# One core, cosine attention into a gated MLP: first-pair norms of four units by a power on GpSimd, and reciprocals of the odd units' sums by ScalarE straight from PSUM

## The chip, the cores and the metric

The kernel runs on one core of one Trainium2 chip. The metric is the device time of one execution in microseconds (us). The core has five engines that run side by side and wait for each other through semaphores: TensorE (PE in the profile; PEld is its weight load), ScalarE (ACT), VectorE (DVE), GpSimd (POOL) and SyncE (SP), whose queue here only issues DMAs. Each engine, and each issuing queue, takes its instructions strictly in the order in which the program holds them.

## The reference

The first part is attention over cosine similarities, the second an MLP with the gate h·cos(h). Eight batches, 12 heads, 448 positions, 64 numbers a head.

```python
q_n = q / (np.linalg.norm(q, axis=-1, keepdims=True) + 1e-06)
k_n = k / (np.linalg.norm(k, axis=-1, keepdims=True) + 1e-06)
scores = np.matmul(q_n, k_n.transpose(0, 1, 3, 2)) / tau
attn = np.exp(scores - max);  attn = attn / (sum(attn) + 1e-09)
attn_out = np.matmul(attn, v)                      # (8, 12, 448, 64)
x = attn_out as (8*448, 12*64)
h = x @ w_in;  g = h * np.cos(h);  out = g @ w_out  # (3584, 768)
```

## The kernel before

**Units and pairs.** The work on heads is cut into 16 units `u` of six heads (half a batch), and each unit into three pairs of heads, numbered `g = 3u + p` from 0 to 47. A batch `b` is units `2b` and `2b + 1`.

**Norms of a unit** (`square`, `reduce`, `rnorm`, `scale`). GpSimd squares q and k of a pair (L617, 1.7 us), VectorE sums the squares over a head (L624), and 1/norm is made in one of two ways. Most units take ScalarE: a `Ln` (L644) and an `Exp` with scale -0.5 (L647), one instruction each for all three pairs of the unit (42 columns). Unit 3 takes GpSimd: it adds 1e-12 (L640) and raises to the power -0.5 (L641), pair by pair (14 columns). GpSimd then multiplies q and k by it (`scale`, L655, 1.7 us a pair, tile `qks`). From pair 9 on, a transposing DMA on SP's queue (L672, labels `T9`, `T10`, ...) brings `qks` into `qkT`, which the scores of that pair read. The norms of unit `u + 1` are made while the pairs of unit `u` are worked on.

**A pair** (`pair`, `scores`, `attend`). TensorE makes the scores of pair `g` in four steps (the first, a narrow one, at L712, three at L704) into two PSUM buffers SC, ScalarE takes the exponential of each (L719, tile `PX`), and TensorE multiplies by the values of pair `g - 1` into PSUM tile AV (L741 and L733; L793 and L809 for the pairs below). The sums over the exponentials, the softmax denominators, are made in two ways. Pairs in `PLAN["direct"]` (0 to 5, 7 to 11, 17, 23, 47) make them beside the product, and ScalarE inverts them from PSUM by `Ln` and `Exp` with scale -1 (L873 and L875; L859 and L861 for pairs 0 to 3). The other pairs of a unit share a count step (`counts`, L765): TensorE multiplies by a matrix of ones at chosen columns (`mark`, L558 to L562), so that each sum lands in a row of AV.

**The chain of a unit** (`counts`, then `chain`). VectorE copies the 128x224 sums out of AV into `xs` (L771). A DMA on SP's queue gathers 16 rows of `xs` (four, where only one pair is left) into `sums`, spread over 128 partitions of 28 columns (L892). VectorE takes the reciprocal (L899; for unit 2 GpSimd, L896). A second DMA writes it to the DRAM buffer `scr` (L900, `spread`), two more read it back, broadcast to 64 partitions each, into `RB` (L902, `bcast`). GpSimd multiplies the unnormalized products `xu` by `RB` into `xT` (L907), one instruction a pair.

**The MLP.** M1 of a batch (`m1`, L920) multiplies `w_in` by `xT`; ScalarE takes a sine with a shift (the cosine, L949) and VectorE the product `g` (L951). M1 of batch `b` stands behind the pair at `points[...]`: pairs 12, 21, 27, 33, 39, 45 for batches 1 to 6, and the end for batch 7. For its sines ScalarE loads another function table (L534) ahead of M1 and the exponential's table behind it, and in between there is no `Ln` or `Exp`. M2 (L1019 in quarters of the array, L1048 whole) multiplies by `w_out`. Its steps are put between the steps of the pairs in counted portions (`m2_fill`), each tile's result is copied out (L983, L986) and stored (L990).

**What sets the order.** The kernel's code lists the operations with what they read and write, and a list scheduler (`Program.arrange`, `play`) then gives each engine its fixed order from estimated costs. Each operation has a latest start (`late`) reckoned backwards from TensorE's own order; an engine other than TensorE takes the ready operation with the earliest `late`. TensorE keeps the written order except that it may look eight steps ahead for one that is ready. So an edit to one operation can move others on any engine.

Of the kernel before, what the change touches and what calls it, by code (L numbers as in the profile page):

```python
# [6 lines left out]
ACT = mybir.ActivationFunctionType  # L7
ALU = mybir.AluOpType
# [5 lines left out]
PLAN = {  # L14
    "apart": 1,
    "ahead": (1, 2),
    "halves": tuple(range(25)),
    "folded": (0, 1, 2, 3),
    "grid": {2: (16, 5, 6), 3: (11, 3, 4), 4: (8, 2, 3)},
    "hold": 0.6,  # L20
    "margin": 1.0,
    "sq": ["AA", "A", "A", "P", "P", "P"],
# [4 lines left out]
    "late4": {1: (7, "T9"), 2: (8, "T10")},  # L27
    "power": (2,),
    "late": 0.0,
    "sooner": {8: 20, 12: 20},  # L30
    "mixed": (3, (3, 0, 1, 2, 0, 1, 2, 0), (2, 3, 4, 0, 1, 5)),
    "turned": 9,
# [9 lines left out]
    "turns": {3: (3, 0, 1, 2, 0, 1, 2, 0)},  # L42
    "lastbank": 2,
    "end": (4, 3, 0),
    "parts": {3: (0, 1, 2, 3), 4: (0, 1, 3)},
    "scaled": {},
    "squared": {(5, 2): "A"},
    "u5": ("gather2", "gather2", "gather2"),
    "tail": 192,
    "twin": 4,  # L50
    "given": {13:(0,0,2,3),16: (4, 0, 5, 2), 22:(1,2,5,6), 26:(3,2,5,6), 27:(0,0,3,2), 34: (12, 4, 5, 6), 46: (12, 4, 3, 4), 47: (4, 0, 5, 0)},
    "roots": (3,),
    "lead": {33: 5, 45: 5, 12: 13, 21: 13},
    "vloads": {3: [(4, "x6"), (5, "x6")], 4: [(6, "x11")], 5: [], 6: [(7, "x15"), (8, "x15")]},
    "behind": {2: 8, 3: 0, 4: 8},
# [340 lines left out]
def bass_cosine_attention__then__act_gcu_kernel(  # L396
# [9 lines left out]
    B, NH, S, D = q.shape  # L406
# [53 lines left out]
    xs = sbs("xs", 2, [128, S // 2], F32)  # L460
    RB = sbs("RB", 2, [128, UP * S], F32)
    sums = sbs("sums", 2, [128, S // 16], F32)
    rcp = sbs("rcp", 2, [128, S // 16], F32)
# [5 lines left out]
    mark = sb("mark", [128, 3 * 4 * 32], BF16)  # L469
    iot = cosb[0].bitcast(I32).ap()[:, 0:128]  # L470
    cst = sb("cst", [128, 4], F32)
# [7 lines left out]
    scr = nc.dram_tensor("scr", (NU, 8 * S), F32)  # L479
# [11 lines left out]
    markv = mark.ap().rearrange("p (k v m) -> p k v m", k=3, v=4)  # L491
# [5 lines left out]
    AVv = AV.ap().rearrange("p (a s) -> p a s", a=2)  # L497
# [13 lines left out]
    def dma(eng, fns, reads, writes, sem, bulk=0.0, label="", behind=None, weight=1.0, pad=0.0):  # L511
        took, descs = 0.75, 0
        for y in ISSUE if eng == "SP" else ():
            if label.startswith(y):
                took, descs = ISSUE[y]
        o = P.op(eng, lambda e: [f(e) for f in fns], reads, writes, cost=took * len(fns), dma=sem, bulk=bulk, label=label)
        o.nd, o.descs, o.lead = len(fns), descs * len(fns), 0.3 if label[0] == "T" else 0.0
        o.weight, o.pad = weight, pad
        if behind is not None:
            P.order_only(behind, o)  # L520
        return o
# [3 lines left out]
    def act(fn, reads, writes, cols, table=None, aps=0, label="", bias=0.0):  # L525
        o = P.op("ACT", fn, reads, writes, cost=0.165 + cols / 1200.0 + 0.09 * aps, label=label, bias=bias)
        if table is not None:
            if last_table[0] is not None:
                P.order_only(last_table[0], o)
            last_table[1].append(o)  # L530
        return o
# [9 lines left out]
    def dve(fn, reads, writes, cycles, lock=False, label="", bias=0.0):  # L541
        return P.op("DVE", fn, reads, writes, cost=0.15 + cycles / 960.0, lock=lock, label=label, bias=bias)

    def pool(fn, reads, writes, cost, label="", bias=0.0):
        return P.op("POOL", fn, reads, writes, cost=cost, lock=True, label=label, bias=bias)
# [13 lines left out]
    for z in range(2):  # L559
        for n, at in enumerate(((0, 24), (0, 16, 24), (8,), (16,))):  # L560
            for x in at:
                dve(lambda e, z=z, n=n, x=x: e.memset(markv[64 * z : 64 * z + 64, 0 : z + 2 : z + 1, n, x : x + 1], 1.0), ["mark0"], ["mark"], 8)  # L562
    sel = [gT.bitcast(F32).ap()[:, (f * RING + S) // 2 : (f * RING + S) // 2 + 128] for f in (NF - 2, NF - 1)]
    for n in range(2):
        dve(lambda e, n=n: e.tensor_scalar(
# [65 lines left out]
    def rnorm(u, p0, p1, t=(0, 1)):  # L631
        i = u % 2
        h, w = slice(2 * p0, 2 * p1), slice(*blocks(t))
        n = (p1 - p0) * 2 * (w.stop - w.start)
        tag = "%d.%d" % (u, p0) + ("" if len(t) == 2 else "ab"[t[0]])
        keys = [(p, z) for p in range(p0, p1) for z in t]
        if u in PLAN["roots"]:
            x, y = n2v[i][:, h, w].rearrange("p h s -> p (h s)"), rnv[i][:, h, w].rearrange("p h s -> p (h s)")
            out_ = [("rn", i, p, z) for p, z in keys]
            pool(lambda e: e.tensor_scalar(y, x, 1e-12, None, ALU.add), [("n2", i, p, z) for p, z in keys], out_, 0.15, label="ad" + tag)  # L640
            pool(lambda e: e.tensor_tensor(y, y, bass.AP(cst, 3, [[4, 128], [0, n]]), ALU.pow), out_ + ["cst3"], out_,  # L641
                 0.05 + 0.166 * n, label="pw" + tag)
            return
        act(lambda e: e.activation(rnv[i][:, h, w], n2v[i][:, h, w], ACT.Ln, bias=cst.ap()[:, 1:2]),  # L644
            [("n2", i, p, z) for p, z in keys] + ["cst1"], [("rn", i, p, z) for p, z in keys],
            n, "E", 1, "ln" + tag)
        act(lambda e: e.activation(rnv[i][:, h, w], rnv[i][:, h, w], ACT.Exp, scale=-0.5),  # L647
            [("rn", i, p, z) for p, z in keys], [("rn", i, p, z) for p, z in keys], n, "E", 0, "rn" + tag)
# [108 lines left out]
    def counts(u):  # L757
        gs = [UP * u + p for p in range(UP) if UP * u + p not in PLAN["direct"]]
        for p, g in enumerate(gs):
            def count(e, p=p, j=g % NPX):  # L760
                v = p + 1 if p else len(gs) == 2
                for c in range(-1, NT3):
                    for o in range(4):
                        a, h = o // 2, o % 2
                        m = e.matmul(AVv[32 * o : 32 * o + 32, 0, 0 : S // 2], markv[:, 0 if c >= 0 else 1 + h, v, :],  # L765
                                     halved(j, c, a, h) if c >= 0 else PHv[j][:, a, :],
                                     start=(p == 0 and c < 0), stop=(p == len(gs) - 1 and c == NT3 - 1))
                return m
            P.op("PE", count, ["mark"] + [("PX", g % NPX, c) for c in range(NT3 + 1)], ["AVa"], cost=(NT3 + 1) * HALF,
                 mode="C32", label="S%d" % g)  # L770
        dve(lambda e: e.tensor_copy(xs[u % 2].ap(), AVv[:, 0, 0 : S // 2]), ["AVa"], [("xs", u % 2)], S // 2, label="xs%d" % u)  # L771

    def attend(g, direct, stages=(0, 1, 2)):
# [112 lines left out]
    def chain(u):  # L886
        i, b = u % 2, u // 2
        n = sum(UP * u + p not in PLAN["direct"] for p in range(UP))
        rows = 16 if n > 1 else 4
        w = rows * S // 256  # L890
        r = rcp[i].ap()[:, 0:w]
        dma("SP", [lambda e: e.dma_start(sums[i].ap()[:, 0:w], bass.AP(  # L892
            xs[i], 0, [[128 // rows * (S // 2), rows], [w, S // 2 // w], [1, w]]))], [("xs", i)], [("sums", i)], "sums%d" % i, 0.7,
            "gather%d" % u, pad=0.0 if u in PLAN["power"] else PLAN["late"]).bias = -PLAN["sooner"].get(u, 0.0)
        if u in PLAN["power"]:
            pool(lambda e: e.tensor_tensor(r, sums[i].ap()[:, 0:w], bass.AP(cst, 2, [[4, 128], [0, w]]), ALU.pow),  # L896
                 [("sums", i), "cst2"], [("rcp", i)], 0.05 + 0.166 * w, label="recip")
        else:
            dve(lambda e: e.reciprocal(r, sums[i].ap()[:, 0:w]), [("sums", i)], [("rcp", i)], 8 * w, label="recip")  # L899
        dma("SP", [lambda e: e.dma_start(bass.AP(scr, u * 8 * S, [[w, 128], [1, w]]), r)],  # L900
            [("rcp", i)], [("scr", u)], "scr", 0.02, "spread%d" % u).bias = -8 if u == 2 else 0.0
        dma("SP", [lambda e, a=a: e.dma_start(  # L902
            RB[i].ap()[64 * a : 64 * a + 64, 0 : n * S].rearrange("p (h x) -> p h x", h=2),
            bass.AP(scr, u * 8 * S + a * rows * S // 4, [[0, 64], [rows * S // 8, 2], [1, n * S // 2]])) for a in range(2)],
            [("scr", u)], [("RB", i, p) for p in range(n)], "RB%d" % i, 3.4 * n / UP, "bcast%d" % u, None, 2.4, 0.5).bias = -8 if u == 2 else 0.0
        for p in range(n):
            f = lambda e, p=p: e.tensor_tensor(  # L907
                xTv[b % 2][:, UP * i + p, :].rearrange("p (s o m) -> p o s m", s=NB, o=2),
                xuv[:, u % 3, p, :].rearrange("p (s o m) -> p o s m", s=NB, o=2),
                bass.AP(RB[i], p * S // 2, [[UP * S, 128], [n * S // 2, 2], [S // 2 // NB, NB], [1, S // 2 // NB]]), ALU.mult)  # L910
            pool(f, [("RB", i, p), ("xa", u % 3, p)], [("xT", b % 2, UP * i + p)], 1.1, label="x%d" % (UP * u + p))
# [392 lines left out]
```

## Time and profile before

| | us |
|---|---|
| median of 3 runs | 420.12 |
| lowest and highest | 419.46, 420.16 |
| the profiled execution | 419.35 |
| its span (first to last instruction) | 417.5 |

Granted TensorE clock of the profiled execution: 1.00.

| engine | busy us | share of the span | instructions |
|---|---|---|---|
| PE | 408.9 | 98% | 6213 |
| PEld | 251.8 | 60% | 6213 |
| ACT | 268.7 | 64% | 374 |
| POOL | 237.0 | 57% | 188 |
| DVE | 201.7 | 48% | 289 |

How to read it: times inside the profile count from the span's start. In a wait line, "A <- B: t, n, m" says that A's engine sat idle for t us in total, n times, at most m us, until B released it. In the chain of the work that ended last, each line is a start, a length and what ran. In the groups, a line has the source line, the engine, the operation, what it writes and reads, the shapes, the count, the busy total and the mean in ns.

### The profile page before, as it was taken

To read this page: it belongs to the slowest core of one execution; us is meant where nothing else is said; L and a number is where in the kernel's file an instruction comes from. 1 tells how busy PE (TensorE), PEld (TensorE's weight loads), DVE (VectorE), ACT (ScalarE), POOL (GpSimd) and SP (SyncE) were. 2 spreads that over 40 slices of the span, in tenths; PEclk is the share of its full clock that TensorE was granted. 3 is DMA by queue.
4 is the path that set the end of the run, shared out by engine and by line. 5 is a ranking of instruction groups with operands and counts; after the bars stand their busy time and mean duration, and the time that the engine had idled before them with its cause. 6 is when DMAs were issued, how large, how long until landed. Compare 5 with 4: busy or idle time off the path is not lost.

```text
span 417.5 us, 13926 instructions
## 1 busy us (share of the span) xinstructions
PE 408.9 (98%) x6213; PEld 251.8 (60%) x6213; DVE 201.7 (48%) x289; ACT 268.7 (64%) x374; POOL 237.0 (57%) x188
## 2 busy tenths in 40 slices
PE   8799999999999999999999999999999999999997
PEld 3354556655666755675567756776567755655565
DVE  4474653446753276334753368333863344413411
ACT  5797578994988647786486647775487745714500
POOL 4999995899556746758475394906857320020000
DMA  7999999999788896979865995959956720141023
GB/s 185 259 255 226 207 209 199 241 135 218 128 113 165 187 195 144 173 152 194 188 130 115 216 231 106 157 107 213 228 98 139 152 69 3 44 119 38 2 71 82
DMA packets 80272, 63.62 MB, mean 152 GB/s; under 512 B 43476, under 2 KB 74452, under 8 KB 80212
## 3 DMA queue, kind: packets, MB, share of 16 engines
q1 hardware_dynamic: 62004, 50.05, 57.2%
q0 software_dynamic: 18048, 12.59, 21.5%
q8 instruction: 49, 0.80, 0.8%
q10 hardware_dynamic: 160, 0.10, 0.1%
q14 instruction: 11, 0.09, 0.1%
HBM read 54.98 MB, written 11.19 MB: 158 GB/s over the span
## 4 chain that ended last, share of the span: by engine, by line
PE 88%; DMA 6%; ACT 3%; DVE 1%; POOL 1%; issue 0%; SPq 0%; ACTq 0%
PE MP L1019 25%; PE SC L920 20%; PE AV L920 12%; PE SC L704 6%; PE AV L741 4%; PE MP L1048 4%; PE AV L765 3%; PE SC L1048 3%; DMA va<-in_v_dram 3%; DMA qkT<-qks 3%; PE MP L920 2%; PE AV L809 2%; PE AV L800 1%; PE SC L712 1%; PE AV L793 1%; ACT cosb L949 1%
## 5 line engine op out<-in xcount | busy, mean ns | idle before, releaser
L719 ACT ACTIVATE PX<-SC 128x448 bf16<-128x448 f32 (+1 forms) x192 | 149.5, 824 | 23.7 <-PE SC L712 13.8
L1019 PE MATMUL MP<-W,gT 64*64 64x384 bf16 x2816 | 138.0, 323 | 0.7 <-DVE qkT L693 0.6
L1019 PEld LDWEIGHTS MP<-W,gT 64*64 64x64 bf16 x2816 | 85.2, 107 | 32.2 <-issue 4.3
L655 POOL TENSOR_TENSOR qks<-raw,rn 128x896 bf16<-128x896 f32 (+1 forms) x48 | 79.7, 1680 | 26.4 <-ACT rn L647 26.2
L920 PE MATMUL SC<-xT,W 128*128 128x448 bf16 x444 | 90.9, 353 | 0.0
L617 POOL TENSOR_TENSOR sq<-raw 128x896 bf16<-128x896 f32 x44 | 73.8, 1690 | 17.9 <-DMA raw<-in_q_dram 16.0
L907 POOL TENSOR_TENSOR xT<-xu,RB 128x448 bf16<-128x448 f32 x34 | 37.9, 1137 | 59.2 <-DMA RB<-scr 59.2
L920 PEld LDWEIGHTS SC<-xT,W 128*128 128x128 bf16 x444 | 43.1, 98 | 40.2 <-ACT osb L983 0.4
L949 ACT ACTIVATE cosb<-SC,cst 128x896 f32<-128x896 f32 x37 | 37.3, 1007 | 38.5 <-PE SC L920 36.6
L920 PE MATMUL AV<-xT,W 128*128 128x448 bf16 x276 | 59.6, 352 | 0.0
L624 DVE TENSOR_REDUCE n<-sq 128x14 f32<-128x896 bf16 (+2 forms) x49 | 51.7, 1058 | 5.6 <-ACT sq L615 5.0
L951 DVE TENSOR_TENSOR gT<-SC,cosb 128x896 bf16<-128x896 f32 x37 | 40.2, 1088 | 26.4 <-ACT cosb L949 26.3
L704 PE MATMUL SC<-qkT 64*64 64x448 bf16 x576 | 52.6, 353 | 0.2
L949 ACT ACTIVATE cosb<-AV,cst 128x896 f32<-128x896 f32 x23 | 23.2, 1007 | 37.0 <-PE AV L920 35.3
L751 DVE COPY xu<-AV 128x448 f32<-128x448 f32 x34 | 21.2, 625 | 45.1 <-PE AV L733 45.1
L920 PEld LDWEIGHTS AV<-xT,W 128*128 128x128 bf16 x276 | 26.6, 98 | 25.3 <-DVE xs L771 1.1
L951 DVE TENSOR_TENSOR gT<-AV,cosb 128x896 bf16<-128x896 f32 x23 | 25.0, 1089 | 26.4 <-ACT cosb L949 26.4
L741 PE MATMUL AV<-PX,va 64*64 64x448 bf16 x408 | 36.7, 349 | 0.0
L986 DVE COPY osb<-MP 128x384 f32<-128x384 f32 x26 | 14.5, 557 | 43.4 <-PE MP L1019 32.1
L591 POOL DMA_DIRECT2D va<-in_v_dram x32 | 21.8, 689 | 6.6 <-DMA raw<-in_q_dram 4.2
L879 POOL TENSOR_TENSOR xT<-xu,RB 128x448 bf16<-128x448 f32 x8 | 9.1, 1138 | 26.4 <-ACT RB L875 26.4
L704 PEld LDWEIGHTS SC<-qkT 64*64 64x64 bf16 x576 | 17.7, 106 | 10.5 <-ACT PX L719 4.0
(82 smaller groups left out, 380.0 us busy)
## 6 DMA issues: line engine op xcount, KB each, us to landing
raw<-in_k_dram SPq DMA_DIRECT2D x48, 224.0 KB, 6.4
raw<-in_q_dram SPq DMA_DIRECT2D x48, 224.0 KB, 7.1
out_dram<-osb SPq DMA_DIRECT2D x54, 192.0 KB, 3.3
va<-in_v_dram POOLq DMA_DIRECT2D x32, 192.0 KB, 8.1
RB<-scr SPq DMA_DIRECT2D x18, 336.0 KB, 4.7
W<-in_moe_w_in_dram POOLq DMA_DIRECT2D x4, 768.0 KB, 14.7
W<-in_moe_w_out_dram POOLq DMA_DIRECT2D x4, 768.0 KB, 19.5
RB<-scr SPq DMA_DIRECT2D x6, 224.0 KB, 3.9
```

The lines of the kernel that those rows point to most:

```text
L617: pool(lambda e, x=x, y=y: e.tensor_tensor(y, x, x, ALU.mult), src_, dst, 0.1 + n * 1.78e-3, label="sq%d.%d" % (u, p)).pad = LATE if u > 1 ...
L624: dve(lambda e, w=w: e.tensor_reduce(out=n2v[i][:, 2 * p : 2 * p + 2, w], in_=sqv[p][:, :, w, :], axis=mybir.AxisListType.X, op=ALU.add), ...
L655: f = lambda e, s0=s0, s1=s1: e.tensor_tensor(qksv[i][:, p, s0:s1].rearrange("p s h d -> p h s d"), rawv[i][:, h, s0:s1, :], bass.AP(rn[i] ...
L704: m = e.matmul(SCv[z][BP * o : BP * o + BP, a, 0:S], t[r, c - 1 + (NT3 + 1) * o, 0:BP], t[r, :, BP : 2 * BP], start=True, stop=True)
L719: act(lambda e: e.activation(PHv[j] if c == 0 else PXv[j][:, c - 1], SCv[z][:, :, 0:n], ACT.Exp, scale=1.0 / TAU), ["SC%d" % z], [("PX", j ...
L741: m = e.matmul(AVv[64 * a : 64 * a + 64, o, 0:S], vav[y][r, 2 * p + a, c + 1, :], PXv[j][r, c, a, :], start=(c == 0), stop=False)
L907: f = lambda e, p=p: e.tensor_tensor(xTv[b % 2][:, UP * i + p, :].rearrange("p (s o m) -> p o s m", s=NB, o=2), xuv[:, u % 3, p, :].rearra ...
L920: t = e.matmul(ph[:, a, 0:S], W1v[:, order[c], 128 * n : 128 * n + 128], xTv[b % 2][:, order[c], :], start=(c == 0), stop=(c == NKC - 1))
L949: act(lambda e, ph=ph, cz=cz: e.activation(cosv[cz], ph[:, :, 0:S], ACT.Sin, bias=cst.ap()[:, 0:1], scale=1.0), names(gi) + ["cst0"], [("c ...
L951: dve(lambda e, ph=ph, cz=cz, gi=gi: e.tensor_tensor(gTv[:, 2 * gi : 2 * gi + 2, S * (b % 2) : S * (b % 2) + S], ph[:, :, 0:S], cosv[cz], ...
L1019: r = e.matmul(POH[b][x : x + 64, 0:HW], gTv[k, y, col + x : col + x + 64], W2v[k, y, HW * b : HW * b + HW], start=(y == 0 and h == 0), st ...
L1048: r = e.matmul(po[:, 0 : w[1] - w[0]], gTv[:, y, col : col + 128], W2v[:, y, w[0] : w[1]], start=(y == 0), stop=(y == NF - 1))
```

## The change

Three things are edited.

1. `PLAN["parts"]` cuts the norm of units 8, 10, 12 and 14 in two: pair 0 by itself, pairs 1 and 2 together. `PLAN["roots"]` sends the first part to GpSimd, as the add and the power of unit 3. ScalarE keeps the second part, now 28 columns.
2. Units 5, 7, 9, 11, 13 and 15 (`PLAN["inverted"]`) lose the copy out of AV, the gather DMA and VectorE's reciprocal. ScalarE reads the sums from PSUM with `Ln` into `xs`, then takes `Exp` with scale -1 in place. `spread` writes 16 rows of `xs` (or four) of 224 numbers each to `scr`, in the layout that `bcast` already reads.
3. Each mark column is repeated over eight columns, so that all 128 rows of AV hold a sum.

```diff
+    "inverted": (5, 7, 9, 11, 13, 15),
+    "bi": 0.0,
...
-    "parts": {3: (0, 1, 2, 3), 4: (0, 1, 3)},
+    "parts": {3: (0, 1, 2, 3), 4: (0, 1, 3), 8: (0, 1, 3), 10: (0, 1, 3), 12: (0, 1, 3), 14: (0, 1, 3)},
...
-    "roots": (3,),
+    "roots": (3, (8, 0), (10, 0), (12, 0), (14, 0)),
...
-  ... e.memset(markv[64 * z : 64 * z + 64, 0 : z + 2 : z + 1, n, x : x + 1], 1.0), ["mark0"], ["mark"], 8)
+  ... e.memset(markv[64 * z : 64 * z + 64, 0 : z + 2 : z + 1, n, x : x + 8], 1.0), ["mark0"], ["mark"], 16)
...
-        if u in PLAN["roots"]:
+        if u in PLAN["roots"] or (u, p0) in PLAN["roots"]:
...
+        if u in PLAN["inverted"]:
+            r, key = xs[u % 2].ap(), ("xs", u % 2)
+            act(lambda e: e.activation(r, AVv[:, 0, 0 : S // 2], ACT.Ln), ["AVa"], [key], S // 2, "E", label="lnS%d" % u, bias=PLAN["bi"])
+            act(lambda e: e.activation(r, r, ACT.Exp, scale=-1.0), [key], [key], S // 2, "E", label="expS%d" % u, bias=PLAN["bi"])
+            return
         dve(lambda e: e.tensor_copy(xs[u % 2].ap(), AVv[:, 0, 0 : S // 2]), ["AVa"], [("xs", u % 2)], S // 2, label="xs%d" % u)
...
+        if u in PLAN["inverted"]:
+            dma("SP", [lambda e: e.dma_start(bass.AP(scr, u * 8 * S, [[S // 2, rows], [1, S // 2]]),
+                                             bass.AP(xs[i], 0, [[128 // rows * (S // 2), rows], [1, S // 2]]))],
+                [("xs", i)], [("scr", u)], "scr", 0.02, "spread%d" % u)
         else:
+            ... gather, reciprocal and spread as before
```

More of the change, by code (lines that the diff above doesn't have):

```diff
@@ L561, in bass_cosine_attention__then__act_gcu_kernel @@
             for x in at:
-                dve(lambda e, z=z, n=n, x=x: e.memset(markv[64 * z : 64 * z + 64, 0 : z + 2 : z + 1, n, x : x + 1], 1.0), ["mark0"], ["mark"], 8)
+                dve(lambda e, z=z, n=n, x=x: e.memset(markv[64 * z : 64 * z + 64, 0 : z + 2 : z + 1, n, x : x + 8], 1.0), ["mark0"], ["mark"], 16)
     sel = [gT.bitcast(F32).ap()[:, (f * RING + S) // 2 : (f * RING + S) // 2 + 128] for f in (NF - 2, NF - 1)]
@@ L890, in chain @@
         w = rows * S // 256
[L891 to L897, printed above, removed]
-        else:
-            dve(lambda e: e.reciprocal(r, sums[i].ap()[:, 0:w]), [("sums", i)], [("rcp", i)], 8 * w, label="recip")
-        dma("SP", [lambda e: e.dma_start(bass.AP(scr, u * 8 * S, [[w, 128], [1, w]]), r)],
-            [("rcp", i)], [("scr", u)], "scr", 0.02, "spread%d" % u).bias = -8 if u == 2 else 0.0
+        if u in PLAN["inverted"]:
+            dma("SP", [lambda e: e.dma_start(bass.AP(scr, u * 8 * S, [[S // 2, rows], [1, S // 2]]),
+                                             bass.AP(xs[i], 0, [[128 // rows * (S // 2), rows], [1, S // 2]]))],
+                [("xs", i)], [("scr", u)], "scr", 0.02, "spread%d" % u)
+        else:
+            r = rcp[i].ap()[:, 0:w]
+            dma("SP", [lambda e: e.dma_start(sums[i].ap()[:, 0:w], bass.AP(
+                xs[i], 0, [[128 // rows * (S // 2), rows], [w, S // 2 // w], [1, w]]))], [("xs", i)], [("sums", i)], "sums%d" % i, 0.7,
+                "gather%d" % u, pad=0.0 if u in PLAN["power"] else PLAN["late"]).bias = -PLAN["sooner"].get(u, 0.0)
+            if u in PLAN["power"]:
+                pool(lambda e: e.tensor_tensor(r, sums[i].ap()[:, 0:w], bass.AP(cst, 2, [[4, 128], [0, w]]), ALU.pow),
+                     [("sums", i), "cst2"], [("rcp", i)], 0.05 + 0.166 * w, label="recip")
+            else:
+                dve(lambda e: e.reciprocal(r, sums[i].ap()[:, 0:w]), [("sums", i)], [("rcp", i)], 8 * w, label="recip")
+            dma("SP", [lambda e: e.dma_start(bass.AP(scr, u * 8 * S, [[w, 128], [1, w]]), r)],
+                [("rcp", i)], [("scr", u)], "scr", 0.02, "spread%d" % u).bias = -8 if u == 2 else 0.0
         dma("SP", [lambda e, a=a: e.dma_start(
```

## The prediction

> **What bounds the kernel now.** I read the busy shares first, then the waits of all engines, then those of TensorE alone, then the chain of work that ended last.
>
> ```profile
> PE 408.9 (98%) x6213; PEld 251.8 (60%) x6213; DVE 201.7 (48%) x289; ACT 268.7 (64%) x374; POOL 237.0 (57%) x188
> ```
>
> ```profile
> POOL xT L907 <- DMA RB<-scr: 59.2, 9, 13.3
> ...
> POOL qks L655 <- ACT rn L647: 26.2, 10, 6.4
> ```
>
> The wait view gives GpSimd 59.2 us for the broadcast reciprocals and 26.2 us for ScalarE's norms: the two waits that the change works on. But GpSimd is not the bound. TensorE is busy in 98% of the span, and the same view for TensorE alone has little:
>
> ```profile
> PE SC L712 <- DMA qkT<-qks: 0.8, 2, 0.6
> ```
>
> That is the one wait of TensorE behind which this change has a step: scores that wait for a transposition. The chain shows where the larger of the two comes from:
>
> ```profile
> 161.57 1.01 ACT cosb L949
> ...
> 162.60 1.28 ACT L534
> ...
> 163.89 0.33 ACT rn L644
> ...
> 164.65 0.14 ACT rn L647
> ...
> 164.86 1.70 POOL qks L655
> ...
> 166.57 6.51 DMA qkT<-qks
> ...
> 173.13 0.29 PE SC L712 x4
> ```
>
> The last sine of M1, the table load, `Ln` and `Exp` of unit 8's norm, the scaling, transposition T24, first score of pair 24. All of it hangs on M1's end, because the norm's `Ln` can't run under the sine table. Its input was there long before: VectorE's sum for pair 0 of unit 8 ended at 151.6.
>
> How long TensorE really stood still is read from starts, since ends are modelled:
>
> ```profile
> 171.37 1.17 PE L1019 MATMUL MP<-W,gT 64*64 64x384 bf16 x24
> 173.13 0.29 PE L712 MATMUL SC<-qkT 64*64 64x224 bf16 x4 [0.59 <-DMA qkT<-qks]
> ```
>
> Elsewhere four such L1019 matmuls start every 0.163 us (20 of them take 0.81 in the chain). So 24 stream for 0.98 and end at 172.36: 0.76 us of standstill before 173.13. The same reckoning ahead of pair 30 (T30 issued at 213.59, landed after 4.61, score at 218.25) gives 0.33. Ahead of pairs 36 and 42, which take the same path, and in all the rest from 85 us on, no other gap between starts is over 0.26; most are about 0.1, where the tiling of the array changes.
>
> **Part 1, the norm by a power.** Durations of what is added and of what stands nearest:
>
> ```profile
> L641 POOL TENSOR_TENSOR rn<-rn,cst 128x14 f32<-128x14 f32 x3 | 7.9, 2619 | 0.2
> ...
> L859 ACT ACTIVATE RB<-AV 128x224 f32<-128x224 f32 x4 | 1.4, 357 | 1.1 <-PE AV L817 1.0
> ...
> L861 ACT ACTIVATE RB<-RB 128x224 f32<-128x224 f32 x4 | 1.6, 390 | 0.1
> ...
> L771 DVE COPY xs<-AV 128x224 f32<-128x224 f32 x13 | 5.1, 392 | 12.5 <-PE AV L765 12.5
> ```
>
> Add 0.27 (L640) and power 2.62: 2.89 us of GpSimd, four times, 11.6 us. ScalarE keeps both its instructions (28 columns took 0.315 and 0.227 against 0.326 and 0.246 for 42), so it gains nothing. Cover on GpSimd: the stretch in which it now waits for loads and for ScalarE, in unit 10's case
>
> ```profile
> 192.84 4.98 POOL L617 TENSOR_TENSOR sq<-raw 128x896 bf16<-128x896 f32 x3
> 202.21 1.68 POOL L617 TENSOR_TENSOR sq<-raw 128x896 bf16<-128x896 f32 x1 [4.39 <-DMA raw<-in_q_dram]
> ...
> 211.87 3.34 POOL L655 TENSOR_TENSOR qks<-raw,rn 128x896 bf16<-128x896 f32 x2 [4.06 <-ACT rn L647]
> ```
>
> 197.8 to 202.2 is idle, the sum for pair 0 is ready at 197.8; add, power and scaling end near 202.5, so only 0.3 us falls on the squares behind. For unit 8 the idle time is 7.0. For units 12 and 14 the squares of units 13 and 15 move back by up to 4.5 (12: 247.2 to 251.7). The last of them would end at 256.8 and 305.4, and the VectorE sums that read them ran at 257.35 and 308.9 anyway. Cost: nothing; without that cover, up to 2.9 us on the next unit's transpositions, which land about 4 us or more ahead of their scores.
>
> What it moves: T24 can issue near 156.5 instead of 166.57, T30 near 203 instead of 213.59. With the longer of their two landings, 6.51, T24 is there at 163 and T30 at 209.5, ahead of the first scores that M2 and the pairs before them leave room for. The scalings of pairs 1 and 2 still wait for ScalarE but go first behind it, 1.7 us sooner. Next late would be T25: about 164.9 + 1.7 + 6.5 = 173.1, and its first score needs pair 24 finished, some 4.5 us after 171.5. So it isn't. Gain: 0.76 + 0.33 = 1.09 us; by the wait view's own count 0.8.
>
> A rule that speaks against a 2.6 us GpSimd instruction is in the Trainium skill, SBUF — State Buffer, on the shared port pair: a GpSimd instruction holds the pair that it shares with VectorE for its whole length and a VectorE instruction with two SBUF inputs is blocked. The trace has VectorE working inside unit 3's power (45.27 to 47.89): the products L951, one PSUM and one SBUF input, took 1.09 and 1.08 against a mean of 1.09. That agrees with the page, which names another kind of operand; no blocked instruction is in the trace.
>
> **Part 2, the odd units' sums.** Removed, six times: VectorE 0.39 (L771) and 0.32 (L899); the gather, 0.60 on SP's queue and 1.8 to landing. Added, six times: ScalarE 0.357 + 0.390 = 0.75, 4.5 us in all. `spread` now moves 16 runs of 896 bytes (8 for half) in place of 128 short ones; not shown before, so its landing lies between the 1.4 and 6.1 us that L900 has, and I take its median 2.4. The chain to `RB` loses some 3 us (unit 9: copy ends 222.9, spread issued at 226.6). That gives GpSimd its operands sooner, but M1 never waited for them: unit 9's last product ended at 239.3, M1, which takes 20 matmuls of 0.189 first, needed it at about 240.6; unit 15's ended at 374.35, ahead of M1's start at 375.5. Gain on the path: nothing.
>
> What may cost: ScalarE is in order, so `Ln` and `Exp` stand ahead of the next pair's exponentials, and AV is free when `Ln` is done instead of the copy. The `Ln` is as long as the copy (0.36 against 0.39). ScalarE just behind the counts of unit 9, which end at 222.5:
>
> ```profile
> 219.59 2.58 ACT L719 ACTIVATE PX<-SC 128x896 bf16<-128x896 f32 x3 [0.46 <-PE SC L704]
> 223.90 0.55 ACT L719 ACTIVATE PX<-SC 128x448 bf16<-128x448 f32 x1 [1.73 <-PE SC L712]
> ```
>
> It is idle for 1.7 us, and so behind units 11 and 13: free. Not free are unit 5 (0.5 idle, then exponentials in a row), unit 7 (its 1.8 idle is the wait for T24, which goes) and unit 15 (0.84 idle, of which 0.32 lies behind the counts). Bounds: from zero, TensorE having M2 steps to do meanwhile, to 0.75 + 0.75 + 0.43 = 1.93. I take 0.2, since in all the profile TensorE's matmuls waited for an exponential once, for 0.5. A gain is excluded: nothing on ScalarE gets shorter.
>
> The Trainium skill, ScalarE: Activation LUTs, tells kernels to take VectorE's reciprocal rather than ScalarE's. It says so for accuracy, of one function, and its timing rule (186 ns and 0.833 a column, overlapping by 93) would make the pair 0.65 us; by it the 1.93 would be lower.
>
> **Part 3.** Fourteen memsets of 64x2 (60 ns alone, 13 in 0.27 us) become 64x16, by the width that the 128x192 memset of L558 (0.22) shows about 0.2 us in all, at 2 us, while the first square starts at 5.2. Nothing.
>
> **The sum.** -1.09 + 0.2 = -0.9. The profiled execution took 419.35 (span 417.5 and 1.85 around it), 0.77 under the median; so 418.45 there, and **419.2** beside the median of 420.12. The scheduler reorders every engine, so I give this case 418.8 to 419.7.
>
> **Rivals.**
> - *ScalarE's new pair becomes the wait* (slower). Place: `exp18`, `exp24` and `exp47`. If all 1.93 reaches TensorE: 420.12 - 1.09 + 1.93 = 421.0. It decides once TensorE has used up its M2 steps before the score buffer is free. For it: 15 weight loads of scores already wait for an exponential, 4.0 us in total; against it: at most 0.5 each, and hidden for TensorE. 18%.
> - *More than the two stalls goes.* With T24 and T30 early, M2 need not be interleaved around a gap. Summed from starts, TensorE's small gaps are 2.07 us in 163 to 189, 1.75 in 210 to 237, 1.46 in 306 to 332.5, but 1.26 in 257.6 to 284.7. All like the best: -0.81 - 0.49 - 0.20 = -1.5, 418.6. Against: most are changes of tiling that stay. 17%.
> - *The wait only changes its name*: T25 or T31, still behind the table load, stalls what T24 did. 420.1. Against: the slack above. 7%.
> - *The power blocks VectorE*, the skill's rule above reaching L951: each of four times one product late by up to 2.6, less the 1.2 us by which a 2.27 us step outlasts it; 4 x 1.4 = 5.6 us, about 425. Against: the 1.09 and 1.08. 3%.
>
> **Numbers.** The forecast has 55%. About 0.2% (0.84 us) is what a measurement of this kernel can tell from no change. The forecast lies just past it: 34 points faster, 21 within. Faster: 34 + 17 = 51%. Same: 21 + 7 = 28%. Slower: 18 + 3 = 21%. The range leaves out the last rival, and the outer parts of the first two (about 16 points): 418.1 to 421.2.
>
> **What would show it.** Right: no wait of TensorE for `qkT` from 163 us on; T24 and T30 issued before M1's table load; power instructions in GpSimd's old idle time; ScalarE's `Ln` on AV about 0.36 and starting within 0.1 us of the counts' end; `RB` landing about 3 us sooner for odd units and no less TensorE work. Wrong: TensorE waiting for `PX` or for ScalarE on AV near pairs 18, 24 and 47, squares of units 9 to 15 so late that their transpositions are waited for, or a new order of M2 with more gaps.

## Result and the profile after

| us | before | after |
|---|---|---|
| median of 6 runs each | 420.09 | 425.08 |
| lowest and highest | 419.39, 422.11 | 423.38, 429.38 |
| the profiled execution | 419.35 | 425.69 |
| its span | 417.5 | 423.9 |

The medians are 5.0 us apart, and the ratio of the runs is 1.0143 (1.0111 to 1.0176): 1.4% slower, where 0.9 us less was forecast. The granted clock of the profiled execution is 0.996.

First the busy shares of the page after:

```profile
PE 410.1 (97%) x6213; PEld 253.1 (60%) x6213; DVE 198.2 (47%) x277; ACT 272.7 (64%) x386; POOL 248.5 (59%) x196
```

Twelve instructions fewer on VectorE, twelve more on ScalarE, eight more on GpSimd: the work moved as written, and TensorE has the same 6213 matmuls in a span 6.4 us longer. So TensorE stands still, or runs slower, somewhere. The stretch of GpSimd's timeline in which pair 0 of unit 8 is normed (start, length, engine, line, operation, shapes):

```profile
152.07 0.26 POOL L642 TENSOR_SCALAR rn<-n 128x14 f32<-128x14 f32 x1 [1.11 <-DVE n L626]
152.41 2.62 POOL L643 TENSOR_TENSOR rn<-rn,cst 128x14 f32<-128x14 f32 x1
155.11 1.69 POOL L657 TENSOR_TENSOR qks<-raw,rn 128x896 bf16<-128x896 f32 x1
```

Here add and power are where they were put, in time that was idle. T24 is issued at 156.82 (forecast 156.5), T30 at 202.13 (203), and the wait view of TensorE has no line for the DMA into `qkT` any more. ScalarE's pair on the odd units' sums, in the view of the tile `xs` (least, median, most ns):

```profile
L775 ACT ACTIVATE xs<-AV x6: 357/358/358, 125.1 to 366.9; 128x224 f32<-128x224 f32 x6
L776 ACT ACTIVATE xs<-xs x6: 382/392/393, 129.6 to 368.0; 128x224 f32<-128x224 f32 x6
```

0.358 and 0.392 against the 0.357 and 0.390 assumed. Both waits for transpositions are gone, and still the profile is 6.4 us longer: something else costs 7.5 us. The waits of TensorE name it, wrongly as will be seen:

```profile
PE MP L932 <- POOL rn L643: 2.9, 1, 2.9
...
PE AV L932 <- DVE gT L963: 0.8, 1, 0.8
...
PE AV L767 <- issue: 0.6, 1, 0.6
```

The first is a single standstill inside the products that open M1 of batch 3. TensorE's timeline there before, and after:

```profile
190.50 1.30 PE L920 MATMUL AV<-xT,W 128*128 128x448 bf16 x6
191.63 0.54 PE L920 MATMUL MP<-xT,W 128*128 128x448 bf16 x2
192.01 0.54 PE L920 MATMUL AV<-xT,W 128*128 128x448 bf16 x2
```

```profile
190.56 1.30 PE L932 MATMUL AV<-xT,W 128*128 128x448 bf16 x6
194.75 0.58 PE L932 MATMUL MP<-xT,W 128*128 128x448 bf16 x2 [2.89 <-POOL rn L643]
195.12 0.95 PE L932 MATMUL AV<-xT,W 128*128 128x448 bf16 x2
```

Its weight loads after:

```profile
191.50 0.10 PEld L932 LDWEIGHTS MP<-xT,W 128*128 128x128 bf16 x1
194.75 0.10 PEld L932 LDWEIGHTS MP<-xT,W 128*128 128x128 bf16 x1 [3.15 <-issue]
```

The weight load for the next matmul stands too, and for it the view knows no releaser ("issue"). A weight load of `W` needs nothing from a norm. The named power ran from 191.39 for 2.62; its end signal at 194.02 is the last event before TensorE moves, and it is for unit 10's scaling. Behind the standstill two matmuls take 0.75 from start to start (194.75, 195.12 at first, then 195.87, 196.62) instead of 0.38: half speed, and the granted clock is 0.50 from 195.1 to 198.5. The stretch in windows (length, then busy time per engine; PEclk is the granted clock):

```profile
185.00:191.00 6.00, 6.00 (x137) 4.56 (x128) 3.56 (x7) 5.23 (x8) 4.79 (x5) 1.00 1.24 166
...
194.00:199.00 5.00, 4.25 (x14) 1.83 (x14) 0.00 (x0) 0.65 (x1) 4.95 (x4) 0.66 1.73 87
```

Now all gaps between TensorE's starts that before doesn't have: 3.06 here, 1.68 for nine matmuls at half speed, and single gaps ending at 77.8 (0.57), 164.55 (0.57), 275.2 (0.73) and 298.34 (0.95). Their sum is 7.56; less the 1.09 of the two waits that went, 6.5. Measured: 6.4. So the whole loss of this execution is TensorE standing still or running at half speed.

**What the standstills have in common.** I counted TensorE's instructions in the trace, all kinds (weight loads, matmuls, semaphores), up to the one that ended each standstill. Three of the gaps above, those ending at 77.8, 194.75 and 275.2, end at number 1985, 6081 and 8641: each is 193 more than a multiple of 256. The page's list of DMA queues has one that carries instructions (packets, MB, share):

```profile
q8 instruction: 49, 0.80, 0.8%
```

49 packets of 16,384 bytes for about 12,550 instructions of TensorE: 256 in each. So TensorE's program reaches it piece by piece, by DMA. In what follows, an edge is the place in the work at which a new packet's instructions begin, and starvation is a standstill because that packet isn't there yet. The packet ahead of number 6081 moved from 192.16 to 193.42, and TensorE went on at 194.75. Before, the packet for the same place moved from 187.64 and was there with 55 instructions still to go, the smallest margin of that profile. After, number 6081 was reached before its packet had landed: TensorE had run out of instructions.

The packet came late; theory S below says that loads of q and k were in its way. SP's queue before, then after:

```profile
181.02 2.55 SPq L902 DMA_DIRECT2D RB<-scr  x2
183.62 0.61 SPq L577 DMA_DIRECT2D raw<-in_k_dram  x1
...
187.65 5.83 SPq L672 DMA_TRANSPOSE qkT<-qks  x2
193.54 0.69 SPq L892 DMA_DIRECT2D sums<-xs  x1
194.27 0.61 SPq L577 DMA_DIRECT2D raw<-in_k_dram  x1
```

```profile
176.80 1.31 SPq L914 DMA_DIRECT2D RB<-scr  x2
...
179.51 0.61 SPq L579 DMA_DIRECT2D raw<-in_k_dram  x1
...
184.27 1.25 SPq L674 DMA_TRANSPOSE qkT<-qks  x1
185.56 0.60 SPq L579 DMA_DIRECT2D raw<-in_k_dram  x1
```

The loads of units 10 and 11 are ordered behind the broadcast of unit 7's reciprocals (`behind` in `load`). That broadcast (`RB<-scr`) is 4.2 us earlier, where some 3 was forecast, and takes the loads with it: unit 10's go out at 179.51 instead of 183.62, unit 11's first at 185.56 instead of 194.27. The loads of unit 10, the first of unit 11 and three transpositions into `qkT` now meet between 178 and 191. When a packet is asked for isn't recorded; in both profiles none starts more than some 290 instructions ahead of its edge. Reckoned from 280 to 290 ahead, this one waits 7.6 to 7.8 us after and 3.1 to 3.3 before, an estimate from the two profiles.

The other two gaps, 164.55 and 298.34, have a chain: VectorE's reciprocal waits for its gather, and a product for TensorE is queued behind it.

```profile
291.31 5.59 DMA sums<-xs
...
296.92 0.04 DVE rcp L911
...
297.17 1.04 DVE gT L963
...
298.34 2.43 PE AV L932 x12
```

### The profile page after: what moved, and what is told of

It is laid out like the page before. It is cut to its first block, busy times and chain, and to the rows that moved or that the text cites. A ratio compares the mean times of both kernels' runs of the same rounds, so it can differ in the third digit from the quotient of the medians.

```text
span 423.9 us, 13923 instructions
## 1 busy us (share of the span) xinstructions
PE 410.1 (97%) x6213; PEld 253.1 (60%) x6213; DVE 198.2 (47%) x277; ACT 272.7 (64%) x386; POOL 248.5 (59%) x196
## 4 chain that ended last, share of the span: by engine, by line
PE 81%; DMA 6%; POOL 3%; SPq 3%; DVE 3%; ACT 2%; issue 1%; ACTq 0%; DVEq 0%; POOLq 0%
PE MP L1031 25%; PE SC L932 16%; PE AV L932 10%; PE SC L706 6%; PE AV L743 4%; DMA sums<-xs 4%; PE MP L1060 4%; PE AV L767 3%; PE SC L1060 3%; PE MP L932 2%; PE AV L816 2%; SPq L579 2%; DVE gT L963 2%; DMA raw<-in_q_dram 1%; POOL qks L657 1%; POOL sq L619 1%
## 5 line engine op out<-in xcount | busy, mean ns | idle before, releaser
L1031 PEld LDWEIGHTS MP<-W,gT 64*64 64x64 bf16 x2816 | 86.1, 107 | 33.1 <-issue 4.9
L932 PE MATMUL AV<-xT,W 128*128 128x448 bf16 x276 | 60.6, 357 | 0.8 <-DVE gT L963 0.8
L706 PE MATMUL SC<-qkT 64*64 64x448 bf16 x576 | 53.6, 353 | 0.2
```

Source lines behind the costliest of these rows:

```text
L706: m = e.matmul(SCv[z][BP * o : BP * o + BP, a, 0:S], t[r, c - 1 + (NT3 + 1) * o, 0:BP], t[r, :, BP : 2 * BP], start=True, stop=True)
L932: t = e.matmul(ph[:, a, 0:S], W1v[:, order[c], 128 * n : 128 * n + 128], xTv[b % 2][:, order[c], :], start=(c == 0), stop=(c == NKC - 1))
L1031: r = e.matmul(POH[b][x : x + 64, 0:HW], gTv[k, y, col + x : col + x + 64], W2v[k, y, HW * b : HW * b + HW], start=(y == 0 and h == 0), st ...
```

## The experiments

Theory S: TensorE starves, because the change puts loads ahead of an instruction packet. Rival R: the wait view is right, and GpSimd's power holds TensorE. Theory V, for the smaller gaps: VectorE, in order, waits for a gather. Each time is a median, and each ratio is against runs of before on the same chip, with its 95% interval. To follow them, here is by how much ScalarE's first sine of M1 of a batch comes later than in before's profile, in the one profiled execution of each kernel:

| us | batch 2 | 3 | 4 | 5 | 6 | end | ratio of the runs |
|---|---|---|---|---|---|---|---|
| before, at | 147.51 | 193.72 | 241.25 | 289.76 | 336.74 | 417.52 | |
| after | 0.34 | 4.63 | 4.45 | 5.18 | 6.34 | 6.34 | 1.0143 |
| e1 power alone | 0.01 | 2.11 | 1.76 | 1.88 | 1.88 | 1.88 | 1.0032 |
| e2 sums alone | -0.04 | 1.23 | 3.18 | 4.16 | 4.16 | 4.15 | 1.0082 |
| e3 after, +152 | 4.51 | 3.74 | 3.56 | 4.00 | 8.18 | 8.18 | 1.0069 |
| e4 after, +76 | 0.38 | -0.39 | -0.69 | -0.08 | 0.13 | 0.14 | 0.9997 |
| e5 small loads | 0.00 | -0.76 | 0.91 | 0.91 | 2.26 | 2.27 | 1.0083 |
| e6 gather 12 later | -0.25 | 3.71 | 5.41 | 5.41 | 5.61 | 5.60 | 1.0079 |
| e7 before, +76 | 0.04 | 0.86 | 0.50 | 0.51 | 0.51 | 0.49 | 1.0026 |
| e9 power, +76 | 0.57 | 1.51 | 1.17 | 1.17 | 1.17 | 1.17 | 1.0013 |
| e10 power, +228 | 0.21 | -0.56 | -0.91 | -0.91 | -0.91 | -0.91 | 1.0018 |
| e11 after, +228 | 1.60 | 0.84 | 1.01 | 1.02 | 1.53 | 1.54 | 1.0079 |
| e12 sums, +76 | -0.61 | -1.23 | 0.46 | 0.46 | 1.17 | 1.17 | 1.0005 |

A profile is one execution, and some lie well off their median: e3's took 427.54 (median 422.77), e6's 424.92 (422.38), e10's 418.54 (421.14), e11's 420.96 (423.54). So the table shows where one execution lost time, and the ratio what the kernel costs. "+76" stands for 76 instructions more at TensorE's start, explained at e3.

**e1: the power alone.** `"inverted": ()`.

> The changed kernel with the odd units' sums put back to copy, gather and VectorE's reciprocal; the power on GpSimd stays. Theory S (TensorE's instruction fetch starves): the 3.06 us standstill ahead of M1 of batch 3 ends exactly when a 16 KB packet on the instruction queue has landed; it started 7.6 us after the point at which such a fetch starts otherwise, because the loads of units 10 and 11 follow bcast7, which the short chain of unit 7 made 4 us earlier, and they fill the DMA rings together with T28. With the long chain back those loads stand as before: no standstill over 0.5 us ahead of M1 of batch 3, time 419.0 to 421.0. Theory R (GpSimd's power is what TensorE waits for, as the wait view says: TensorE <- POOL rn 2.9 us): the power of unit 10 is still there, the standstill stays at 2 to 4 us, time 423 to 426.

Measured 420.79, 1.0032 (1.0007 to 1.0057). The same instruction, number 6081, waits 2.87 us, with the same power beside it:

```profile
PE MP L932 <- issue: 2.7, 1, 2.7
```

Here the view puts no releaser to it. The time fell into S's range and the standstill into R's. My reading of S, that without part 2 the loads stay late, was wrong: unit 10's go out at 179.3. With unit 8's first transposition gone from this stretch, SP's list has unit 7's spread ahead of the next transposition and its broadcast (177.95) ahead of an output store, where before's has them the other way round (spread 178.39, store 179.84, broadcast 181.02).

**e2: the sums alone.** `"roots": (3,)`, and `"parts"` as before.

> The changed kernel with the norms of units 8, 10, 12 and 14 put back to ScalarE; the odd units' reciprocals stay on ScalarE from PSUM. Theory S: bcast7 is early, so the loads of units 10 and 11 are early too; but without the power T29 stands ahead of all loads of unit 11, so a part of the crowding goes: standstill ahead of M1 of batch 3 between 0 and 3 us, time 420 to 424. Theory R: no power, no standstill, time 419.5 to 420.5. The wait of 0.76 us for T24 comes back under both.

Measured 423.36, 1.0082 (1.0048 to 1.0116). Time and standstill are as S had them. There is no power at this place, and number 6081 still waits, 1.66 us:

```profile
190.07 1.30 PE L932 MATMUL AV<-xT,W 128*128 128x448 bf16 x6
192.87 0.54 PE L932 MATMUL MP<-xT,W 128*128 128x448 bf16 x2 [1.49 <-issue]
```

R has fallen: the power isn't needed for the standstill. Unit 10's loads go out at 179.3 here too. Two more gaps (1.86 at 239.0, 0.88 at 289.3) end at 193 past a multiple of 256.

**e3, e4, e11: the same kernel at another place of the packets' edges.** The matmuls that keep TensorE busy in the first 15 us are cut into two (e4), three (e3) or four (e11): 76, 152 or 228 instructions more, all before 15.1 us. Behind that, every engine's order stays.

```diff
-    P.filler = (lambda e, shut: e.matmul(PO[:, 0:S], zt[:, 0:128], zt, start=shut, stop=shut), zero, MM, 0.3)
+    CUTS = (0, 224, 448)      # e3: (0, 150, 300, 448); e11: (0, 112, 224, 336, 448)
+    P.filler = (lambda e, shut: [e.matmul(PO[:, a:b], zt[:, 0:128], zt[:, a:b], start=shut, stop=shut) for a, b in zip(CUTS, CUTS[1:])][-1], zero, MM, 0.3)
```

> The changed kernel, each of TensorE's 38 filler matmuls at the start (448 columns of zeros) cut in three (150, 150, 148): 152 more instructions on TensorE, the same columns, and nothing else is touched. All three standstills of over 0.5 us that no dependency explains (ending at 77.8, 194.75 and 275.2) stand at instruction 193 modulo 256 of TensorE's stream. Theory S: the edge of the 256 instructions moves by 152, that is 104 later in the work; M1 of batch 3 has its edge then about 104 instructions, some 10 us, later, after the fetch has landed: the standstill of 3.06 us and the 1.7 us of half-speed matmuls behind it go, time 419.5 to 421.5, and any new standstill stands at 193 modulo 256 of the new stream. Theory R: nothing changes, 423 to 426.

> The changed kernel, each filler matmul cut in two (224, 224): 76 more instructions on TensorE, the edge 76 earlier in the work. Theory S: the stream runs out 76 instructions sooner, at the end of the pairs ahead of M1 of batch 3 (about 188.8), while the fetch is asked for only 1.5 us sooner: a standstill of 1 to 5 us remains, but about 76 instructions earlier in the work, time 422 to 427. Theory R: the standstill stays at the same place in the work, at the 13th matmul of M1, with its 3 us; time 423 to 426.

> The changed kernel, each filler matmul cut in four: the edge 28 later in the work. Theory S: the 3.06 us ahead of M1 of batch 3 shrinks by 2.6 to about 0.5 and the half-speed matmuls go, 420 to 422, with the small losses (unit 12's reciprocal 0.95, other fetches 0.5 to 1.5) still there. Rival: 423 to 426.

e4: 419.82, 0.9997 (0.9978 to 1.0015), 5.3 us below after with the same work. The forecast of a remaining standstill was a miss, and the time lies under both ranges: by the reckoning above the packet was asked for at 182.5, two microseconds sooner, and waited 2.6.

```profile
190.10 1.30 PE L932 MATMUL AV<-xT,W 128*128 128x448 bf16 x6
191.24 0.54 PE L932 MATMUL MP<-xT,W 128*128 128x448 bf16 x2
```

No gap, while the power, the early loads and the pair on ScalarE are all in this kernel. From batch 2 to 3 it gains 0.77 us on before and from 3 to 4 another 0.30, where 0.76 and 0.33 were forecast for T24 and T30; starvations of 1.05 at 81.7 and 0.60 at 284.2 take it back.

e3: 422.77, 1.0069 (1.0045 to 1.0094), outside both ranges. In its profile, the slowest of its seven executions, the gap ahead of batch 3 is gone (4.51 to 3.74), as S has it, but another edge fell badly: 2.50 at 76.7, followed by half speed, and late in the span V's wait:

```profile
PE MP L1031 <- issue: 2.5, 2, 2.3
...
PE AV L932 <- DVE gT L963: 2.1, 1, 2.1
```

e11: 423.54, 1.0079 (1.0051 to 1.0107). The gap ahead of batch 3 shrank to 0.53 as expected, with 1.54 at 74.1 instead; the median missed the 420 to 422 and lies in the rival's 423 to 426.

**e5: the loads of units 10 and 11 small.** They move a seventh of their bytes (one block of each head), so the numbers behind them are others; everything is issued as before.

```diff
+ ... [1, D if u in (10, 11) else NB * D]])
+ ... rawv[i][BP * x : BP * x + BP, h, 0 : (1 if u in (10, 11) else NB)] ...
```

> The changed kernel, every instruction in the order it had, but the loads of q and k of units 10 and 11 move one seventh of the bytes (one block of 64 columns of seven; the squares and scalings of these units then read six blocks of older data). Theory S in its first form (the bytes of these loads hold the instruction fetch up): the fetch that is needed ahead of M1 of batch 3 starts 1 to 4 us after its trigger instead of 7.6, the 2.9 to 3.1 us standstill at instruction 6081 is gone, time 420 to 422.5 (the wait of 0.95 us ahead of M1 of batch 5 and small ones elsewhere stay). Rival form (the transpositions T28 and T29, 224-byte-wide work of their own, hold it up): they are unchanged, the standstill stays at 1.5 us or more, time 422.5 to 425.

Measured 422.39, 1.0083 (1.0056 to 1.0109), within S's range, with this at the place:

```profile
189.73 1.30 PE L932 MATMUL AV<-xT,W 128*128 128x448 bf16 x6
190.87 0.54 PE L932 MATMUL MP<-xT,W 128*128 128x448 bf16 x2
```

The edge is where it was, the loads start as early, only most of their bytes are gone, and the standstill with them: the packet starts at 188.02 instead of 192.16 and lands with 18 instructions to go. Batch 3 comes 0.76 sooner than before. That is S's other half; the transpositions (their packets have 256 bytes in the trace, not 224) don't hold TensorE up by themselves, though the packet still waits longer than before's. The time gained less than the standstill was worth: starvation moved to 236.7 (1.60), and V's wait to 294.3 (1.16).

**e6: unit 12's gather planned 12 us longer**, so that the scheduler puts its reciprocal behind more of VectorE's products: `pad={12: 12.0}.get(u, PLAN["late"])` in its DMA.

> The changed kernel with one planned latency raised: the scheduler counts 12 us more for unit 12's gather, which moves VectorE's reciprocal of unit 12 from ahead of the first product of M1 of batch 5 to behind the sixth, spread12 behind T42 and six GpSimd instructions; TensorE's and ScalarE's orders are unchanged. Theory V (the 0.95 us ahead of the 13th... matmuls of M1 of batch 5 is VectorE standing in order at this reciprocal until the gather, 5 us in the queue, has landed): the gap of 0.95 us at 298.3 goes, VectorE's wait for the gathers falls by 2.3 us, time 0.7 to 1.2 us under the changed kernel's, 423 to 425. Rival (the gap is VectorE's load of products as such): it stays, time as the changed kernel. The standstill at instruction 6081 stays under both.

Measured 422.38, 1.0079 (1.0048 to 1.011), under the forecast's 423. The wait of the reciprocals fell from 6.2 (after) to 1.9, and the step from batch 5 to 6 from 1.16 to 0.20:

```profile
PE MP L932 <- POOL rn L643: 2.9, 1, 2.9
...
DVE rcp L911 <- DMA sums<-xs: 1.9, 1, 1.9
...
PE AV L767 <- issue: 1.5, 1, 1.5
```

The gap went with the move, as V has it. That the gather's wait alone makes it is not shown: in e4 the order is after's, the reciprocals wait 8.2 in all, and TensorE has no such gap. The large standstill is untouched, 3.07 with half speed behind it, and a new one of 1.63 at 241.2 is at 193 past a multiple of 256.

**e8: e4 with the gathers of units 6 and 12 planned later** (4 and 12 us).

> The changed kernel with the filler matmuls cut in two (e4) and both gathers' planned latencies raised (unit 6 by 4 us, unit 12 by 12), a version meant to keep the gain of 1.09 us. Theories S and V: e4's profile was 1.07 us ahead of before at M1 of batch 4 and lost 0.60 to a fetch at 284.2; without VectorE's waits 418.5 to 420.0. If moving unit 6's reciprocal shifts the loads and a fetch comes late again: 420 to 423.

Measured 420.55, 1.0025 (1.0002 to 1.0049): nothing gained on e4, and within the forecast's second range, for fetches that come late again. Its profiled execution, 425.79, is 5 us above the median; it has four starvations, of 0.6, 0.8, 1.9 and 2.0, all at 193 past a multiple of 256.

**e7: before, +76.** e4's edit in the kernel before.

> The kernel before, each of its filler matmuls cut in two: 76 more instructions on TensorE and nothing else. In its profile the fetch ahead of M1 of batch 3 landed with 55 instructions left, the smallest margin of all. Theory S: with the edge moved, other fetches become the tight ones; the time moves by up to 2 us either way with no other edit, 418.5 to 422, any standstill of over 0.3 us behind 70 us without a dependency at 193 modulo 256. Rival (76 small matmuls more cost or change nothing of note, and the edge doesn't matter for this kernel): 419.7 to 420.3 and the gaps of before.

Measured 420.25, 1.0026 (1.0007 to 1.0046). Before, which had no such gap, gets 1.69 at 189.5 and 0.50 at 81.4:

```profile
PE AV L765 <- issue: 1.5, 1, 1.5
...
PE AV L809 <- issue: 0.3, 1, 0.3
```

So the starvation isn't the change's own, and at the one other alignment that was tried before is no faster than the changed kernel at that alignment (e4).

**e9, e10: the power alone, +76 and +228.**

> The power on GpSimd alone (as e1), with the 38 filler matmuls cut in two. e1 lost 2.87 us at instruction 6081 and was otherwise 1.1 us ahead of before at M1 of batch 4. Theory S: with the edge 76 earlier, as in e4, the fetch ahead of M1 of batch 3 comes in time; the gain of the two waits for transpositions stays, 418.0 to 419.5, 0.998 to 0.996 of before. Rival (shifting the edge only happened to suit e4): a standstill of 1 to 3 us at 193 modulo 256 elsewhere, 420 to 422.

> The power on GpSimd alone, each filler matmul cut in four of 112 columns: 228 more instructions, the edge 28 later in the work. Theory S: in M1, where some 10.6 instructions are run in a us, 28 are 2.6 us; of e1's 2.87 us at M1 of batch 3 at most 0.5 is left, and no half-speed matmuls behind it; 418.2 to 420. Rival: as e1, 420.5 to 421.5.

e9: 420.15, 1.0013 (0.9995 to 1.0031), with 1.70 at 190.2 and 0.78 at 81.9. S's number was a miss, and the rival came true: the shift that suited e4 doesn't suit this kernel, though its gaps are at 193 past a multiple of 256 too. e10: 421.14 (418.50 to 424.88), 1.0018 (0.9988 to 1.0048). Its profiled execution took 418.54 and has one starvation of 0.45:

```profile
span 416.6 us, 14159 instructions
```

That is 0.9 below before's span, what was forecast for this change; the median isn't there but in the rival's range, 420.5 to 421.5.

**e12: the sums alone, +76.**

> The odd units' reciprocals on ScalarE alone (as e2), the filler matmuls cut in two. e2 lost 1.66, 1.86 and 0.88 us at 193 modulo 256. Theory S: the first two are moved or gone, the waits for T24 and T30 stay, and the part itself is worth nothing: 419 to 421. Rival (ScalarE's new pair costs time of its own): 421 to 424, with TensorE waiting for PX or for AV near pairs 18, 24 and 47.

Measured 419.93, 1.0005 (0.9986 to 1.0023). That is within S's range. Without the power a wait for `qkT` is back (T30's, 2.05 at 218.7; none for T24), there is no starvation over 0.25 us, and ScalarE's pair costs nothing that can be seen:

```profile
PE SC L714 <- DMA qkT<-qks: 1.9, 1, 1.9
...
PE AV L932 <- DVE gT L963: 0.6, 1, 0.6
```

**All together.** In 13 profiles (all but e8's) 23 gaps of over 0.25 us behind 70 us end at 193 past a multiple of 256; of the others, each has a transposition, a product of VectorE or a change of the array's tiling ahead of it. No version is faster than before; e4 has the lowest median, and can't be told from before.

## Why the prediction was wrong

- **The waits on `qkT`, 1.09: right.** T24 and T30 went out within 0.9 us of the forecast and no score waited. T30's agreement is in part luck: it stands in a span that is already 4.5 us late, and its loads came early. Where the starvation stays away, the gain is seen at its size: 0.77 and 0.30 in e4, 0.77 and 0.35 in e10's profile, against 0.76 and 0.33.
- **The power's cover: right in its place, wrong in its step.** Unit 8's power, 2.62, ran in idle time, and the waits of TensorE show no transposition that came late. "Cost: nothing" looked at GpSimd's queue and its consumers alone. Moving T24 also reorders SP's queue, and unit 10's loads go out 4 us sooner by that alone (e1: 179.3 instead of 183.6), with 2.87 us of starvation.
- **ScalarE's pair, +0.2: nothing was seen of it.** TensorE waits for exponentials 0.4 in all against 0.5 before, and e12 has no wait for ScalarE that before doesn't have. Of the two bounds, zero held.
- **"Gain on the path: nothing" of the sooner `RB`: the step that failed.** I asked whether M1 waits for `RB`, and it doesn't. I didn't ask what is ordered behind the broadcast: the loads of units 10 and 11, whose move by 4 and 9 us fills the DMA queues just where TensorE's next instructions are to be fetched. That step's term was 0; it measured 3.06 + 1.68 = 4.74 in after's profile. Either part alone brings unit 10's loads forward (e1 and e2: 179.3) and starves TensorE at this edge (2.87 and 1.66), so the "Cost: nothing" of part 1 failed in the same way, and the 4.74 is the loss of both together.
- **No term for fetching instructions.** The sum treated every gap of TensorE as one of data. The profile before had the queue of 49 packets on its page and one packet that came with 55 instructions to spare; neither was read. The Trainium skill, Runtime: NRT & Kernel Launch, Instruction fetch mechanics, says that instructions come in 16 KiB blocks of 256 and that crossing a boundary is "mostly hidden". The trace agrees on the 16,384 bytes and the 256, and differs on hidden: up to 3.07 us here.
- **VectorE's waits for gathers, 0.57 and 0.95: not foreseen.** I counted the removed gathers and reciprocals as free, not that the even units' remaining ones move ahead of products on VectorE. For the second, e6 has the gap gone with the move, but e4 has it gone without. The first is read from the chain alone, and no other profile with VectorE's order there (e3 to e6, e11) has it over 0.25: it is one execution's.
- **The rivals.** None of the four is what happened: the slower end was given to ScalarE's pair (421.0) and to the power on VectorE (425). The latter's time is close to the result, by chance: the products that ran inside the new powers took 1.03 to 1.09 us, as elsewhere.

Shown: the standstill at batch 3 is starvation (e2 and e4 against R) and goes with the loads' bytes (e5) or with the edge (e4). What TensorE still had in store isn't recorded; it is inferred from the count and from the packets' landing. Not shown: which packets are late in the executions that weren't profiled; e10's median is 2.6 us above its profile. Their mean clocks tell of half speed alone: it is 0.995 or 0.996 in the profiles with one stretch of it, as in four of after's six executions, and 0.999 or more in those with none, as in the other two, which still took 423.38 and 424.47. The 0.57 at 77.8 lies ahead of 122 us, where the engines' orders don't yet differ from before's, so it is put down to the execution and not to the change (e1 has 0.50 there, e6 none over 0.25).

## What to carry to other kernels

When a step makes a buffer or a broadcast ready sooner, list the DMAs ordered behind it and look what else uses the queues at that time; a transfer that starts sooner can cost more than the wait that was removed. In a kernel bound by TensorE, count its instructions and look whether unexplained gaps come at one remainder of 256: if they do, compare versions at several alignments (a few harmless instructions at the start) before a difference of 1% is believed. A releaser in the wait view is an inference: ask whether the waiting instruction reads anything from it.

## What the hardware showed

- **Alignment alone moves the median by 1.3%.** The same change at +0, +76, +152 and +228 instructions: 425.08, 419.82, 422.77, 423.54, with ratios to before of 1.0143, 0.9997, 1.0069 and 1.0079. In each, starvation comes at other places of the work.
- **Half speed after short standstills.** After 3.06 (after), 3.07 (e6) and 2.50 (e3) of starvation, and after a 2.29 wait for VectorE (e3), the granted clock was 0.50 for 3.4 us, and the next eight or nine matmuls went 0.372 apart instead of 0.187; after 2.87 in e1 it stayed 1.00. In the traces the granted clock changes in steps of 3.41 us, and what differs is how a standstill falls on them: TensorE was busy for 0.5 us (after, e6), 1.1 and 1.3 (e3) of the step ahead of the half clock, while e1's standstill fell on two steps with 2.0 and 2.1 each. No step with 1.6 or more of work, from 22 us on, was followed by the half clock in any profile. The Trainium skill, TensorE: Matmul & The Clock Gate, Part 1, has the slow clock after an idle window of about 3.4 us; here 2.3 was enough once.
